# Masked attention, experts and feed-forward in one kernel: the first heads' loads in the order of their use, and the second head's bucket bits ahead of the others'

## The chip, the cores and the metric

The kernel runs on one core of one Trainium2 chip. The metric is the device time of one execution in microseconds (us): the median of three runs. The engines named here are PE (TensorE, matrix products), DVE (VectorE), ACT (ScalarE), POOL (GpSimd) and SP (SyncE, which issues most of the DMA transfers). Every engine works through a list of its own in a fixed order; an instruction that waits for a semaphore holds up all that stand behind it on its engine, and this holds for SP's list of DMA issues too.

## The reference

Three stages follow one another: attention with a mask from hashed buckets, a mixture of experts with one expert per token, and a dense feed-forward h·relu6(h+3)/6. Only the attention stage is touched by the change:

```python
# q, k, v: (2 batches, 8 heads, 768, 64); proj: (64, 6)
q_bits = (einsum('bhsd,dk->bhsk', q, proj) > 0)      # six bits a row
k_bits = (einsum('bhsd,dk->bhsk', k, proj) > 0)
mask   = q_bucket[:, :, :, None] == k_bucket[:, :, None, :]
scores = scale * q @ k.T
scores = where(mask, scores, -1e9)
scores = scores - max(scores, axis=-1)
attn   = exp(scores);  attn = attn / (sum(attn) + 1e-9)
return attn @ v
```

The 1536 rows of the result are the tokens; `x @ w_gate` picks one of 8 experts for each (512 to 1024 to 512, at most 384 tokens an expert), and the feed-forward (512 to 2048 to 512) comes last.

## The kernel before, in words

There are 16 heads (2 x 8), of 768 rows each. The attention stage has 96 steps, six of them for each head: step k handles one block of 128 keys against all 768 queries of its head. What a head needs stands in four tiles of a set (there are four sets, used in turn): X and Y on the side of the queries, K1 and K2 on that of the keys. The data are split in a high and a low half (`hi`, `lo`) for precision; rows 64 to 75 of X and K2 hold the bucket bits as +-numbers, so that a matching bucket adds a constant to the product, and row 76 holds the row's maximum against a row of -1.

Work of one head, in the order in which it is needed:

- `load_r(h)` (L308) loads q and k of a head, 393 kB. `prep(h)` makes `hi` on ACT (L319) and `lo` on DVE (L335), or for the heads in the table entry `ap` on ACT and POOL (L332, L333), and copies them by DMA from SBUF to SBUF into X and K2 (L321, L322) and K1 and Y (L325, L326, L336, L337).
- `bits(g)` handles the bits of four heads: dots with the projection into PSUM (`psb`, L358), signs on DVE into the tile `b` (L347). `put_bits(h)` copies them into X and K2 by two DMAs (L343, L344). Head 0 has its bits made apart at the start.
- `mx(n)` is one block of 128 rows for the row maxima: two matmuls (`psm`, L385) and two maxima on DVE (L388). After the sixth block of a head the six are reduced to `top` (L391), and a DMA sends it to X's row 76 (L392). A table (`ac`) says how many such blocks run ahead in the first steps.
- `scores(k)`: matmuls L402 and L403 into `pst`, exp on ACT (L404) to `pf`; then a high half on ACT (L412) and a low half on POOL (L418), and four steps later, for two steps together, `pv` (L430 to L432) into `psv`.
- For each group of four heads: `load_v(g)` (L510, 786 kB), the largest |v| on DVE (`vmax`, L514), and a power of two from it (`vscale`): the maxima `am` (L523, L525) are transposed on PE (`psn`, L531), reduced (L534) and laid on a diagonal (`dg`, L537), spread over the partitions by PE (`pso`, L540), and turned to scales on DVE (L544 to L559). The `sc` of it scales v (`vsplit`, L636 to L642), and the first call also scales the gate's weights `wg_sb` (L558).
- `load_vt(r)` (L480) loads v of two heads, transposed, into `vt`, of which there is one buffer; `vgate(r)` multiplies it with the scaled gate's weights on PE (`psg`, L491), read by DVE (L500, L501). The next `load_vt` waits for those matmuls.
- `heat` (L283) puts matmuls into the list that compute nothing that is used; the table entry `hn` says how many stand ahead of the steps and in each of the first eight.

The PSUM tiles of `psn`, `pso`, `psg` and later `psb` share one buffer; `psm` has three, `pst` two.

The order on every engine is that in which the program emits its instructions. The head of the stage is written out (its loads, head 0's bits and six blocks of maxima, the first `vscale`); for the 96 steps a table `Q` gives the step, in quarters, at which each part is due, and `spread(k, gen, d)` emits the parts of a generator from step k on, d steps apart. So the table and the written-out head set SP's list as well.

Of the kernel before, what the change touches and what calls it, by code (L numbers as in the profile page):

```python
# [9 lines left out]
F32 = mybir.dt.float32  # L10
F32R = mybir.dt.float32r
# [40 lines left out]
def moe_attention_kernel(ctx, tc, qk, v, vt, pj, wg, w1, w2, win, wout, out, cap):  # L52
    nc = tc.nc
    pe, act, dve, pool, sp = nc.tensor, nc.scalar, nc.vector, nc.gpsimd, nc.sync
# [3 lines left out]
    def opened(stack, name, bufs, side="left", **kw):  # L58
        return stack.enter_context(tc.tile_pool(name=name, bufs=bufs, side=side, reuse_waits="tile", **kw))

    def f32(t):
        return t.bitcast(F32)

    def run(gen):
        for _ in gen:
            pass
# [191 lines left out]
                )  # L258


    Q = {'v': (-3.25, -4.75, -1.75, -2.25), 'vg': (-4.5, -4.75), 'vgd': 1, 'pr': (-13.0, -12.75, -12.0, -12.5), 'prd': 0.6, 'b0': 7.75, 'b': 1.75, 'bd': 0.5, 'vm0': (8.0, 8.25, 10.75, 13.0), 'vm': (-0.5, 4.75, 7.0, 12.25), 'vs': 13.25, 'pa': 1.5, 'ev': 0.5, 'lvt': -5.0, 'v4': (2.0, 3.75, 4.0, 16.25), 'vg0': (1.85, -4.4, 7.75), 'p2': 3.5, 'lr': (0, 3, 1.5, 4.5), 'lv': 5.5, 'vsd': 0.75, 'ac': (0, 0, 2, 6, 7, 8, 9, 10), 'hd': (3, 5, 17), 'hn': (4, 4, 2, 2, 4, 3, 0, 0, 0), 'ap': (0,), 'h0': (7,), 'hl': (4,), 'l0': (), 'll': (1, 10), 'ht': (5, 9)}


    with ExitStack() as actx:
        pa = opened(actx, "pa", 1)
        pr = opened(actx, "pr", 6)
        ph = opened(actx, "ph", 1)
# [3 lines left out]
        ps_v = opened(actx, "ps_v", 2, space=PSUM)  # L271
# [31 lines left out]
        def misc(name):  # L303
            return ps_x.tile([P, 512], F32, tag="x", name=name)

        def load_r(h):
            rt[h] = pr.tile([P, S], F32, tag="r", name=f"r{h}")
            sp.dma_start(out=rt[h], in_=qk[h])  # L308

        def prep(h, first=False):  # L310
# [28 lines left out]
        def put_bits(h):  # L339
            st = sets[h % 4]  # L340
            b = b_t[h // 4]
            o = 32 * (h % 4)
            sp.dma_start(out=f32(st["X"])[D : D + 12], in_=f32(b)[o : o + 12])  # L343
            sp.dma_start(out=f32(st["K2"])[D : D + 12], in_=f32(b)[o + 12 : o + 24])  # L344

        def signs(out, ps, c):
            dve.tensor_scalar(out=out, in0=ps, scalar1=0.0, scalar2=c, op0=ALU.is_gt, op1=ALU.subtract)  # L347

        def bits(g, tiles=None):

            b_t[g] = ph.tile([P, S], F32R, tag="b", name=f"b{g}", bufs=2)
            ps = [None] * 2

            def dot(n, i):
                if i == 0:
                    ps[n] = tiles[n] if tiles else misc(f"psb{g}{n}")
                c = slice(n * HS, (n + 1) * HS)
                pe.matmul(  # L358
                    ps[n][32 * i : 32 * i + 32, :HS], pj_sb[:, 0:32], rt[4 * g + i][:, c], start=True, stop=True
                )  # L360

            def rows(n):
                signs(b_t[g][:, n * HS : (n + 1) * HS], ps[n][:, :HS], cst_sb[:, 0:1])

            if tiles:
                for i in range(4):
                    for n in range(2):
                        dot(n, i)
                    yield
            for n in range(2):  # L370
                if not tiles:
                    for i in range(4):
                        dot(n, i)
                    yield
                rows(n)
                if not tiles:
                    yield

        def mx(n):
            h, c = divmod(n, NC)  # L380
            st = sets[h % 4]
            mm = mxs[h % 2]
            for n in range(2):
                ps = ps_m.tile([P, 512], F32, tag="m", name=f"psm{h}{c}{n}")
                pe.matmul(  # L385
                    ps[:, :HS], st["X"][0:76, c::NC], st["K2"][0:76, n * HS : (n + 1) * HS], start=True, stop=True
                )
                dve.tensor_reduce(out=mm[:, c, n : n + 1], in_=ps[:, :HS], axis=AX.X, op=ALU.max)  # L388
            if c == NC - 1:

                dve.tensor_reduce(out=top[:, h], in_=mm, axis=AX.X, op=ALU.max)  # L391
                sp.dma_start(out=f32(st["X"])[76:77, :].rearrange("o (p c) -> o p c", c=NC), in_=f32(top)[:, h])  # L392

        def scores(k):
            h, j = divmod(k, NC)
# [82 lines left out]
        def load_vt(r):  # L478
            vt_t[r] = pt.tile([P, S], F32, tag="vt", name=f"vt{r}", bufs=1)
            sp.dma_start(out=vt_t[r], in_=vt[r])  # L480
# [169 lines left out]
        load_r(0)  # L650
        act.dma_start(out=pj_sb, in_=pj)
        dve.memset(wg_sb, 0.0)
        for h in range(1, 4):
            load_r(h)
        load_v(0)
        load_vt(0)
        for i in range(2):
            act.dma_start(out=wg_sb[i * D : (i + 1) * D, :, i], in_=wg[i * D : (i + 1) * D])
        st, r0 = sets[0], rt[0]
        dve.tensor_scalar(out=st["X"][0:D], in0=r0[0:D], scalar1=SC, scalar2=None, op0=ALU.mult)  # L660
        act.activation(st["K2"][0:D], r0[D:P], AF.Copy, scale=SC)
        pre = [prep(h, h == 0) for h in range(3)]
        for n in range(2):
            for i, t in enumerate(("X", "K2")):
                c = slice(n * HS, (n + 1) * HS)
                ps = (ps_m, ps_t)[i].tile([P, 512], F32, tag="mt"[i], name=f"psf{n}{i}")
# [4 lines left out]
                signs(st[t][D : D + 12, c], ps[D : D + 12, :HS], cst_sb[D : D + 12, i : i + 1])  # L671
        run(pre[0])
        next(pre[1])
        for i in range(4):
            pool.dma_start(out=f32(sets[i]["K2"])[76:77], in_=neg)
        consts()
        pool.dma_start(out=xd[0:1, :], in_=zrow[:, :DM])
        DOT = (5,)
        b0 = bits(0, [ps_v.tile([P, 512], F32, tag="v", name=f"psb0{n}") for n in range(2)])
        for n in range(NC):  # L680
            mx(n)
            if n in DOT:
                next(b0)
        heat(ps_t, "t", Q["hn"][0])
        for i in range(4):
            vmax(0, i)
        vs = vscale(0)
        next(vs)
        next(vs)
        run(b0)  # L690
        next(vs)
        put_bits(1)
        run(pre[1])
        next(pre[2])
        put_bits(2)

        heat_t.clear()
        STEPS = NC * NH
        AC = (0,) + Q["ac"]
        AHEAD = [range(NC + AC[i], NC + AC[i + 1]) for i in range(8)]  # L700
        END = 2 * NC

        def on_dve(k):
            if k < END:
                return k in Q["h0"]
            return k - STEPS + END in Q["hl"] if k >= STEPS - END else k % 24 in Q["hd"]
# [92 lines left out]
        h = NH - 1  # L799
# [229 lines left out]
    def heat(n):  # L1029
# [21 lines left out]
        out=gates, in0=ps2[:, :, NW:], scalar=1.0 / LS, in1=gates, op0=ALU.mult, op1=ALU.add  # L1051
# [288 lines left out]
```

## Time and profile before

| | us |
| --- | --- |
| median of the runs | 718.79 (717.63 to 719.08) |
| profiled execution, device time | 712.88 |
| its span in the profile | 711.1 |
| PE busy in that span | 682.9 (96%) |
| start of the first `scores` | 19.28 |
| start of the first `pv` | 40.36 |

The span is what the profile shows from the first instruction to the last, and all times of rows are counted from its start. The profiled execution lies 5.91 below the median of the timed runs. The mean granted TensorE clock is 0.983 of full speed. In the rows below a line like "14.10 1.92 DVE L514 ... x4" says that four instructions of line 514 began at 14.10 us and took 1.92 us together; the bracket at its end is the idle time of the engine before it, and who ended it. Rows with "SPq" are DMA issues: the time is that of the issue, not of the transfer.

### The profile page before, as it was taken

The numbers are of one execution on the slowest core, as the hardware profiler recorded it, in microseconds if no ns is written. First come the engines' busy times: TensorE is split into PE (matmuls) and PEld (weight loads), VectorE is DVE, ScalarE is ACT, GpSimd is POOL, SyncE is SP. The second block draws the span as 40 slices with busy tenths as digits, with TensorE's granted clock in tenths as the row PEclk, the third lists the DMA queues.
The fourth block names the chain that finished last, engine by engine and source line by source line (L and its number), as shares of the span: only waits on it lengthen the run. The fifth ranks groups of instructions, "written<-read, shape, count | busy, mean of one in ns | idle before, by whom it ended". The sixth has DMA issues, their size and how long they took to land. (4 is left out here: it accounts for less than half of the span.)

```text
span 711.1 us, 14232 instructions
## 1 busy us (share of the span) xinstructions
PE 682.9 (96%) x5528; PEld 598.2 (84%) x5528; DVE 503.5 (71%) x988; ACT 376.8 (53%) x713; POOL 260.6 (37%) x202
## 2 busy tenths in 40 slices
PE   7999999999998699999999998999999999999996
PEld 2689898898897489999999996788888888888885
DVE  6778889889999788778777785888888632222320
ACT  3468869778779366655666642333333442223420
POOL 4347877977982411110110001333333423311212
PEclk8789999999999999999999999999999999999999
DMA  7585855746480376666665543234333000000001
GB/s 224 120 227 130 239 141 156 226 127 167 98 230 25 115 238 223 218 208 209 209 213 189 193 150 123 89 128 137 121 119 118 1 17 29 30 16 1 0 30 59
DMA packets 37841, 94.14 MB, mean 132 GB/s; under 512 B 7576, under 2 KB 13720, under 8 KB 37760
## 3 DMA queue, kind: packets, MB, share of 16 engines
q1 hardware_dynamic: 34672, 85.71, 40.2%
q0 software_dynamic: 2400, 7.36, 3.1%
q8 instruction: 46, 0.75, 0.4%
q14 instruction: 35, 0.29, 0.1%
q10 hardware_dynamic: 688, 0.03, 0.1%
HBM read 67.14 MB, written 6.29 MB: 103 GB/s over the span
## 5 line engine op out<-in xcount | busy, mean ns | idle before, releaser
L418 POOL TENSOR_TENSOR plo<-pf,phi 128x768 f16<-128x768 f32 x86 | 146.7, 1728 | 60.6 <-ACT phi L412 25.9
L996 POOL TENSOR_TENSOR ib<-wi,ia 128x512 fp32r<-128x512 f32 x32 | 50.1, 1566 | 230.1 <-ACT ia L995 230.1
L388 DVE TENSOR_REDUCE mx<-psm 128x1 f32<-128x384 f32 x192 | 96.3, 548 | 20.1 <-PE psm L385 19.8
L404 ACT ACTIVATE pf<-pst 128x384 f32<-128x384 f32 x192 | 83.4, 486 | 48.9 <-PE pst L403 47.5
L135 DVE TENSOR_TENSOR wl<-raw,wh 128x512 fp32r<-128x512 f32 x128 | 86.7, 688 | 10.2 <-ACT wh L134 3.7
L1223 ACT ACTIVATE rl<-psg,b 128x512 f32<-128x512 f32 x64 | 37.3, 582 | 94.6 <-PE psg L1221 94.5
L1221 PE MATMUL psg<-yTh,ia 128*128 128x512 f32 (+1 forms) x256 | 86.4, 338 | 0.7 <-DVE rl L1224 0.2
L1224 DVE SCALAR_TENSOR_TENSOR rl<-rl,psg 128x512 f32<-128x512 f32 x64 | 35.1, 550 | 73.3 <-ACT rl L1223 73.3
L1221 PE MATMUL psg<-yTh,ib 128*128 128x512 f32 (+1 forms) x256 | 85.9, 335 | 0.0
L1221 PE MATMUL psg<-yTl,ia 128*128 128x512 f32 (+1 forms) x256 | 85.7, 335 | 0.0
L134 ACT ACTIVATE wh<-raw 128x512 fp32r<-128x512 f32 x128 | 77.3, 623 | 2.1 <-issue 1.5
L1243 PE MATMUL pso<-cl,gh 128*128 128x512 f32 x192 | 76.7, 399 | 0.5 <-POOL cl L996 0.5
L402 PE MATMUL pst<-Y,K 128*128 128x384 f32 x192 | 75.1, 391 | 2.0 <-ACT pf L404 2.0
L1243 PE MATMUL pso<-ch,gl 128*128 128x512 f32 x192 | 75.5, 393 | 0.0
L1243 PE MATMUL pso<-ch,gh 128*128 128x512 f32 x192 | 75.5, 393 | 0.0
L412 ACT ACTIVATE phi<-pf 128x768 f16<-128x768 f32 x85 | 71.7, 844 | 1.9
L978 PE MATMUL psy<-hh,wh 128*128 128x224 f32 x256 | 71.3, 279 | 0.0
L385 PE MATMUL psm<-K,X 76*128 76x384 f32 x192 | 66.8, 429 | 4.3 <-DVE mx L388 3.5
L978 PE MATMUL psy<-hl,wh 128*128 128x224 f32 x256 | 70.2, 274 | 0.0
L978 PE MATMUL psy<-hh,wl 128*128 128x224 f32 x256 | 70.1, 274 | 0.0
L403 PE MATMUL pst<-X,K 77*128 77x384 f32 x192 | 66.2, 345 | 0.0
L432 PE MATMUL psv<-vh,plo 128*128 128x73 f16 x576 | 63.6, 196 | 1.7 <-DVE plo L418 1.7
(204 smaller groups left out, 1642.6 us busy)
## 6 DMA issues: line engine op xcount, KB each, us to landing
raw<-in_w_dram SPq DMA_DIRECT2D x64, 512.0 KB
rc<-in_win_dram SPq DMA_DIRECT2D x16, 512.0 KB
rc<-in_wout_dram SPq DMA_DIRECT2D x16, 512.0 KB
r<-in_qk_dram SPq DMA_DIRECT2D x16, 384.0 KB
K<-hi SPq DMA_DIRECT2D x31, 192.0 KB
vr<-in_v_dram SPq DMA_DIRECT2D x4, 768.0 KB
vt<-in_vt_dram SPq DMA_DIRECT2D x8, 384.0 KB
Y<-hi SPq DMA_DIRECT2D x16, 192.0 KB
```

The lines of the kernel that those rows point to most:

```text
L134: act.activation(wh[e, i][:, c], r, AF.Copy)
L135: lo.tensor_tensor(out=wl[e, i][:, c], in0=r, in1=f32(wh[e, i])[:, c], op=ALU.subtract)
L385: pe.matmul(ps[:, :HS], st["X"][0:76, c::NC], st["K2"][0:76, n * HS : (n + 1) * HS], start=True, stop=True)
L388: dve.tensor_reduce(out=mm[:, c, n : n + 1], in_=ps[:, :HS], axis=AX.X, op=ALU.max)
L402: pe.matmul(ps[:, :HS], st["K1"][:, kc], st["Y"][:, qc], start=True, stop=False)
L403: pe.matmul(ps[:, :HS], st["K2"][0:77, kc], st["X"][0:77, qc], start=False, stop=True)
L404: act.activation(pf.rearrange("k (c n p) -> k c n p", c=NC, n=2)[:, :, n], ps[:, :HS].rearrange("k (p c) -> k c p", c=NC), AF.Exp, scale=0 ...
L412: act.activation(phi_t[k], pf_t[k], AF.Copy)
L418: eng.tensor_tensor(out=plo_t[k], in0=pf_t.pop(k), in1=phi_t[k], op=ALU.subtract)
L978: pe.matmul(ps, l, r, start=n == 0, stop=n == 3 * KF - 1)
L1221: pe.matmul(ps, l, x, start=n == 0, stop=n == 3 * KD - 1)
L1243: pe.matmul(po[blk][s], l, r, start=first and n == 0, stop=last and n == 2)
```

## The change

At the start only r of heads 0 and 1 is loaded; r of heads 2 and 3 and v of the first group are issued after head 0's K1 and Y and head 1's X and K2 copies, and the first transposed v after that of head 2's first part. At once after head 0's maxima the dots of head 1 alone are made and their bits sent; those of heads 2 and 3 are made from step 0.25 on (`bits` takes a range of heads), and head 2's are sent at step 2.5 (head 3's, as before, in its `prep`). `top` of head 0 is sent from ACT's queue. Head 1's `lo` moves from DVE to ACT and POOL. In the table, `vm0` (the maxima of v of the second group), `lr` (r of heads 4 to 7) and `lv` (v of the second group) become later, the parts of the first `vscale` stand half a step apart from step 0 on instead of being partly written out ahead, head 1's maxima begin a step earlier, and `hn` falls from 19 to 12 matmuls in all.

```diff
-Q: 'vm0': (8.0, 8.25, 10.75, 13.0), 'lr': (0, 3, 1.5, 4.5), 'lv': 5.5, 'vsd': 0.75, 'ac': (0, 0, 2, 6, 7, 8, 9, 10), 'hn': (4, 4, 2, 2, 4, 3, 0, 0, 0), 'ap': (0,)
+Q: 'vm0': (10.25, 11.0, 11.75, 13.0), 'lr': (2, 3.5, 4.5, 5.5), 'lv': 6.5, 'vsd': 0.5, 'ac': (0, 2, 4, 6, 7, 8, 9, 10), 'hn': (6, 2, 2, 1, 1, 0, 0, 0, 0), 'ap': (0, 1)
...
-        def bits(g, tiles=None):
+        def bits(g, heads=range(4), tiles=None):
...
+            p = slice(32 * heads[0], 32 * heads[-1] + 32)
...
             def rows(n):
-                signs(b_t[g][:, n * HS : (n + 1) * HS], ps[n][:, :HS], cst_sb[:, 0:1])
+                signs(b_t[g][p, n * HS : (n + 1) * HS], ps[n][p, :HS], cst_sb[p, 0:1])
...
-                sp.dma_start(out=f32(st["X"])[76:77, :].rearrange("o (p c) -> o p c", c=NC), in_=f32(top)[:, h])
+                (sp if h else act).dma_start(out=f32(st["X"])[76:77, :].rearrange("o (p c) -> o p c", c=NC), in_=f32(top)[:, h])
...
-        for h in range(1, 4):
-            load_r(h)
-        load_v(0)
-        load_vt(0)
+        load_r(1)
...
         next(pre[1])
+        load_r(2)
+        load_r(3)
+        load_v(0)
...
-        DOT = (5,)
-        b0 = bits(0, [ps_v.tile([P, 512], F32, tag="v", name=f"psb0{n}") for n in range(2)])
+        b0 = bits(0, [1], [ps_v.tile([P, 512], F32, tag="v", name=f"psb0{n}") for n in range(2)])
         for n in range(NC):
             mx(n)
-            if n in DOT:
-                next(b0)
+        run(b0)
+        put_bits(1)
+        run(pre[1])
         heat(ps_t, "t", Q["hn"][0])
         for i in range(4):
             vmax(0, i)
         vs = vscale(0)
         next(vs)
-        next(vs)
-        run(b0)
-        next(vs)
-        put_bits(1)
-        run(pre[1])
         next(pre[2])
-        put_bits(2)
+        load_vt(0)
...
         spread(0, vs, Q["vsd"])
+        spread(0.25, bits(0, [2, 3]), 0.5)
+        at(2.5, put_bits, 2)
```

Three places show how this moves instructions. SP's list at the start, before (r, vr, vt: loads of q and k, of v, of the transposed v; K, X, Y: the tiles of the sets; `b`: the bits):

```order
L308 DMA r_156<-in_qk_dram 128x768
L308 DMA r_160<-in_qk_dram 128x768
L308 DMA r_162<-in_qk_dram 128x768
L308 DMA r_164<-in_qk_dram 128x768
L510 DMA vr_166<-in_v_dram 128x1536
L480 DMA vt_169<-in_vt_dram 128x768
L325 DMA K_129<-hi_187 64x768
L326 DMA Y_128<-hi_187 64x768
```

and now:

```order
L325 DMA K_129<-hi_178 64x768
L326 DMA Y_128<-hi_178 64x768
L336 DMA K_129<-lo_179 64x768
L337 DMA Y_128<-lo_179 64x768
L321 DMA X_131<-hi_188 64x768
L322 DMA K_134<-hi_188 64x768
L308 DMA r_193<-in_qk_dram 128x768
L308 DMA r_195<-in_qk_dram 128x768
L510 DMA vr_197<-in_v_dram 128x1536
L343 DMA X_131<-b_262 12x768
```

The two loads of r and the load of v now stand behind six copies of 64x768 from SBUF to SBUF; ahead of these rows there are only r of heads 0 and 1. Further down SP's list, around the second load of the transposed v, before (X_135 and K_138 are head 2's X and K2):

```order
L326 DMA Y_136<-hi_300 64x768
L343 DMA X_135<-b_264 12x768
L344 DMA K_138<-b_264 12x768
L308 DMA r_325<-in_qk_dram 128x768
L480 DMA vt_354<-in_vt_dram 128x768
L308 DMA r_356<-in_qk_dram 128x768
L392 DMA X_131<-top 1x128x6
```

and now:

```order
L326 DMA Y_136<-hi_290 64x768
L480 DMA vt_297<-in_vt_dram 128x768
L480 DMA vt_346<-in_vt_dram 128x768
L308 DMA r_394<-in_qk_dram 128x768
L343 DMA X_135<-b_262 12x768
L344 DMA K_138<-b_262 12x768
L392 DMA X_131<-top 1x128x6
```

Head 2's bits stood ahead of the second load of `vt` and stand now behind it and behind one load of r. DVE's list in the first `vscale`, before:

```order
L534 TENSOR_REDUCE am_289<-psn_279 2x1
L537 TENSOR_TENSOR dg<-am_289,ident 2x2
L335 SCALAR_TENSOR_TENSOR lo_198<-r_160,hi_197 128x768
L544 COPY am_340<-pso_323 128x2
```

and now (`mx_148` are the maxima of head 1):

```order
L534 TENSOR_REDUCE am_316<-psn_311 2x1
L537 TENSOR_TENSOR dg<-am_316,ident 2x2
L388 TENSOR_REDUCE mx_148<-psm_333 128x1
L388 TENSOR_REDUCE mx_148<-psm_336 128x1
L388 TENSOR_REDUCE mx_148<-psm_339 128x1
L388 TENSOR_REDUCE mx_148<-psm_342 128x1
L347 TENSOR_SCALAR b_262<-psb_313,pj_sb 64x384
L544 COPY am_353<-pso_348 128x2
```

The second half of `vscale` (from L544 on) now stands behind four of head 1's twelve maxima and one half of the bits of heads 2 and 3; L335 of head 1 is gone.

## Rows read from the trace of the kernel before

**Rows 1.** The page: busy time of TensorE, share of the span, instructions.

```profile
PE 682.9 (96%) x5528; PEld 598.2 (84%) x5528; DVE 503.5 (71%) x988; ACT 376.8 (53%) x713; POOL 260.6 (37%) x202
```

**Rows 2.** Windows: length, busy time by engine, granted clock, DMA share, GB/s.

```profile
19.28:26.54 7.26, 5.60 (x29) 3.50 (x26) 6.76 (x17) 5.09 (x10) 3.43 (x2) 1.00 0.46 114
26.54:34.99 8.45, 8.44 (x29) 6.34 (x29) 5.87 (x14) 2.16 (x4) 3.29 (x2) 0.58 0.75 155
34.99:41.50 6.51, 6.51 (x36) 5.26 (x36) 4.10 (x10) 4.76 (x9) 1.65 (x1) 0.50 0.82 237
41.50:45.00 3.50, 3.50 (x44) 3.25 (x42) 2.55 (x7) 2.56 (x6) 2.14 (x2) 1.00 1.01 313
...
100.00:200.00 100.00, 98.17 (x1188) 89.23 (x1188) 88.42 (x203) 81.03 (x151) 81.96 (x55) 1.00 0.57 151
```

**Rows 3.** Windows of the first transfers: loads, then copies.

```profile
9.00:11.00 2.00, 2.00 (x5) 1.32 (x5) 2.00 (x5) 0.00 (x0) 1.93 (x5) 0.95 1.03 389
11.20:14.00 2.80, 2.80 (x7) 1.47 (x7) 2.77 (x6) 0.00 (x0) 2.05 (x12) 0.50 1.04 224
```

**Rows 4.** Timeline of SP: start, time of the issue, what is issued.

```profile
10.17 0.95 SPq L322 DMA_DIRECT2D K<-hi  x1
14.21 0.52 SPq L392 DMA_DIRECT2D X<-top  x1
...
21.57 0.74 SPq L344 DMA_DIRECT2D K<-b  x1
...
35.26 0.34 SPq L480 DMA_DIRECT2D vt<-in_vt_dram  x1
35.64 0.43 SPq L308 DMA_DIRECT2D r<-in_qk_dram  x1
```

**Rows 5.** Waits of SP from 13.9 to 45 us: total, times, longest.

```profile
SPq L480 <- PE psg L491: 5.4, 1, 5.4
```

**Rows 6.** Timeline of DVE.

```profile
14.10 1.92 DVE L514 TENSOR_REDUCE am<-vr 128x1 f32<-128x384 f32 x4
...
19.44 1.14 DVE L347 TENSOR_SCALAR b<-psb,pj_sb 128x384 fp32r<-128x384 f32 x2 [3.09 <-PE psb L358]
20.50 0.27 DVE L534 TENSOR_REDUCE am<-psn 2x1 f32<-2x128 f32 x1
...
21.08 0.96 DVE L335 SCALAR_TENSOR_TENSOR lo<-r,hi 128x768 fp32r<-128x768 f32 x1
21.96 0.15 DVE L544 COPY am<-pso 128x2 f32<-128x2 f32 x1
...
25.93 1.94 DVE L388 TENSOR_REDUCE mx<-psm 128x1 f32<-128x384 f32 x4
29.69 3.81 DVE L388 TENSOR_REDUCE mx<-psm 128x1 f32<-128x384 f32 x8 [1.81 <-PE psm L385]
33.53 0.17 DVE L391 TENSOR_REDUCE top<-mx 128x6 fp32r<-128x18 f32 x1
```

**Rows 7.** Timeline of PE.

```profile
13.27 2.77 PE L358 MATMUL psb<-r,pj_sb 128*32 128x384 f32 x4
...
17.85 1.50 PE L358 MATMUL psb<-r,pj_sb 128*32 128x384 f32 x12
...
23.93 0.98 PE L385 MATMUL psm<-K,X 76*128 76x384 f32 x3
26.54 0.56 PE L385 MATMUL psm<-K,X 76*128 76x384 f32 x1 [1.63 <-DVE mx L388]
...
35.06 0.67 PE L402 MATMUL pst<-Y,K 128*128 128x384 f32 x1
...
36.49 1.50 PE L283 MATMUL heatv<-idle_sb 128*128 128x512 f16 x3
37.44 1.20 PE L385 MATMUL psm<-K,X 76*128 76x384 f32 x2
...
40.36 0.28 PE L430 MATMUL psv<-vh,phi 128*128 128x73 f16 x1
```

More of the change, by code (lines that the diff above doesn't have):

```diff
@@ L258, in windows @@
                 )
-    Q = {'v': (-3.25, -4.75, -1.75, -2.25), 'vg': (-4.5, -4.75), 'vgd': 1, 'pr': (-13.0, -12.75, -12.0, -12.5), 'prd': 0.6, 'b0': 7.75, 'b': 1.75, 'bd': 0.5, 'vm0': (8.0, 8.25, 10.75, 13.0), 'vm': (-0.5, 4.75, 7.0, 12.25), 'vs': 13.25, 'pa': 1.5, 'ev': 0.5, 'lvt': -5.0, 'v4': (2.0, 3.75, 4.0, 16.25), 'vg0': (1.85, -4.4, 7.75), 'p2': 3.5, 'lr': (0, 3, 1.5, 4.5), 'lv': 5.5, 'vsd': 0.75, 'ac': (0, 0, 2, 6, 7, 8, 9, 10), 'hd': (3, 5, 17), 'hn': (4, 4, 2, 2, 4, 3, 0, 0, 0), 'ap': (0,), 'h0': (7,), 'hl': (4,), 'l0': (), 'll': (1, 10), 'ht': (5, 9)}
+    Q = {'v': (-3.25, -4.75, -1.75, -2.25), 'vg': (-4.5, -4.75), 'vgd': 1, 'pr': (-13.0, -12.75, -12.0, -12.5), 'prd': 0.6, 'b0': 7.75, 'b': 1.75, 'bd': 0.5, 'vm0': (10.25, 11.0, 11.75, 13.0), 'vm': (-0.5, 4.75, 7.0, 12.25), 'vs': 13.25, 'pa': 1.5, 'ev': 0.5, 'lvt': -5.0, 'v4': (2.0, 3.75, 4.0, 16.25), 'vg0': (1.85, -4.4, 7.75), 'p2': 3.5, 'lr': (2, 3.5, 4.5, 5.5), 'lv': 6.5, 'vsd': 0.5, 'ac': (0, 2, 4, 6, 7, 8, 9, 10), 'hd': (3, 5, 17), 'hn': (6, 2, 2, 1, 1, 0, 0, 0, 0), 'ap': (0, 1), 'h0': (7,), 'hl': (4,), 'l0': (), 'll': (1, 10), 'ht': (5, 9)}
     with ExitStack() as actx:
@@ L347, in signs @@
             dve.tensor_scalar(out=out, in0=ps, scalar1=0.0, scalar2=c, op0=ALU.is_gt, op1=ALU.subtract)
-        def bits(g, tiles=None):
-            b_t[g] = ph.tile([P, S], F32R, tag="b", name=f"b{g}", bufs=2)
+        def bits(g, heads=range(4), tiles=None):
+            if g not in b_t:
+                b_t[g] = ph.tile([P, S], F32R, tag="b", name=f"b{g}", bufs=2)
+            p = slice(32 * heads[0], 32 * heads[-1] + 32)
             ps = [None] * 2
             def dot(n, i):
-                if i == 0:
+                if i == heads[0]:
                     ps[n] = tiles[n] if tiles else misc(f"psb{g}{n}")
@@ L362, in rows @@
             def rows(n):
-                signs(b_t[g][:, n * HS : (n + 1) * HS], ps[n][:, :HS], cst_sb[:, 0:1])
[L365 to L369, printed above, removed]
-            for n in range(2):
[L371 to L375, printed above, removed]
+                signs(b_t[g][p, n * HS : (n + 1) * HS], ps[n][p, :HS], cst_sb[p, 0:1])
+            for n in range(2):
+                for i in heads:
+                    dot(n, i)
                 if not tiles:
                     yield
+                    rows(n)
+                    yield
+            if tiles:
+                yield
+                rows(0)
+                rows(1)
         def mx(n):
```

## The prediction

> **What bounds the kernel now.** I read the page first: PE is busy for 96% of the span [rows 1], so whatever moves the moment from which PE runs without waits moves the end. Then windows over the first 200 us, to see where that moment is. From 41.50 on PE is busy all the time at full clock, and still for 98.17 of 100 us between 100 and 200 us [rows 2]; before 41.50 it waits, or runs at the lower of its two levels (0.50 between 34.99 and 41.50). The change touches only this stretch. Behind it the lists of PE hold the same work in the same order, and its loads (r of heads 4 to 7, v of the second group) are used 20 and more steps after they are issued. So I ask by how much the first `pv` (40.36 [rows 7]) and what follows come later or sooner, and carry that to the end in full.
>
> Then the timelines of SP, DVE and PE side by side. The chain that leads to 40.36 goes through DVE: `vmax` of v at 14.10, bits at 19.44, `vscale`'s second half from 21.96 to 25.93, then the twelve maxima of head 1, up to its `top` at 33.53 [rows 6]. PE follows its last maxima with `vgate`, reaches step 4 at 35.06, and head 2's first maxima (`psm`) at 37.44 [rows 7]. SP, meanwhile, waited 5.4 us in the issue of the second `vt` for `vgate` [rows 5], until 35.26 [rows 4].
>
> **The change, part by part.**
>
> *v of the first group comes later.* Before, it stood fifth in SP's list, and `vmax` began at 14.10 without waiting. Now SP issues r2, r3 and v0 only after the copy of 10.17 (0.95 long [rows 4]), so from 11.12 on: 393 + 393 + 786 kB = 1.573 MB. At the 389 GB/s of the loads this is 4.0 us, at the 224 GB/s of the copies 7.0 [rows 3]. Earliest end: 11.12 + 4.0 = 15.1. Latest: 11.12 + 7.0 plus 1.6 for the start (below) = 19.7. I take the loads' rate, with 1.6 for the start and half a copy (197 kB at 224 GB/s is 0.9) in front: 17.2. DVE cannot begin before 16.7 anyway: the second dot of head 1 ends where the two dots of 13.27 do, at 16.04 [rows 7], and its eviction (0.57, half of the 1.14 for two [rows 6]; that one of 32 partitions takes as long is an estimate) ends near 16.7. So `vmax` begins at 17.2 (16.7 to 19.7) instead of 14.10.
>
> A rule speaks to this rate. The Trainium skill, "DMA: Bandwidth & Descriptors", section "Bandwidth", says that transfers between HBM and SBUF are bound by the HBM side and those inside SBUF by a faster fabric (some 435 GB/s). The trace has it the other way round: loads at 389, copies at 224 [rows 3]. By the page the copy in front would be gone 0.2 us sooner, and the sum below would be 0.2 less.
>
> *`vscale`, first half.* 17.2 + 1.92 [rows 6] + 0.4 for two small reductions (twice `top`'s 0.17) = 19.5. Transposing 0.3 (an estimate), then L534 and `dg` in 0.6 (20.50 to 21.08 [rows 6]): done at 20.4, which is 0.7 sooner than before, since the bits of heads 1 to 3 are no longer in front. The late v is paid out of a wait of 3.09 before the evictions [rows 6]. PE gets to the first scores at 16.04 + 6 heats of 0.32 (36.49 to 37.44, three [rows 7]) = 18.0, instead of 19.28, but that gains nothing, because PE then stands waiting for `am`.
>
> *`vscale`, second half.* This is the first loss. In DVE's list four maxima of head 1 and half of the bits now stand between `dg` and L544. In PE's list behind the transposition: two dots for heads 2 and 3 (the 1.50 for 12 records [rows 7] are two halves of three heads, so 0.75), step 1's scores 0.8 (step 4 at the low clock took 35.06 to 36.49, 1.43 [rows 7], about half at full), two heats 0.4, the first `psm` 0.4 (0.98 for three [rows 7]). So the first maximum at 19.5 + 0.3 + 2.35 = 22.2; four of them 1.94, half of the bits 0.57: 24.7. `pso` shares its PSUM buffer with `psb`, so it starts then; 0.6 for it and the way back: L544 at 25.3, not 21.96. From L544 to the end of the chain 3.97 (21.96 to 25.93 [rows 6]): 29.3. Eight maxima 3.81, the other half of the bits 0.57, and a gap for PE's scores of step 3: before it was 1.81 [rows 6], now the bits and one heat instead of four cover a part, I take 0.8 (0 to 1.8). With 0.1 for each of four hand-overs: `top` at 34.9 against 33.53, **+1.4**. L335 of head 1 (0.96 [rows 6]) is gone from DVE, but the two more evictions (1.14) have its place. On POOL, which did nothing there, `lo` is free; if POOL were late, K1's copies of head 1 still have until step 6. The ends: +0.1 (v0 in time, no gap) and +4.9 (v0 2.5 later, gap 1.8).
>
> *Head 2's bits.* This is the second loss, and a new wait. `vgate` follows head 1's last maxima as before, so step 4 begins 1.4 later too. Before, step 4 to head 2's first `psm` took 2.38, of which 0.95 were three heats (36.49 to 37.44 [rows 7]); those are now gone, but the copies of the bits, which had been issued long ahead, stand behind the second `vt`, and that waits for `vgate` [rows 5]. In the times of before: issue of `vt` at 35.26, r up to 36.07, then two bit copies of 0.74 each with 0.08 between [rows 4]: 37.7. The landing takes between nothing and 1.6: head 1's last copy ended its issue at 22.31 [rows 4], and its reader ran at 23.93 [rows 7]. In front of them lie 786 kB of `vt` and r, 2.0 us at 389 GB/s, 3.5 at 224 [rows 3]; begun 1.6 after 35.26 they are through at 38.9 or 40.4. So `psm` at 37.7 to 40.9; with the loads' rate and 0.3 for the bits' own 74 kB I take 39.2: **+1.8** (+0.3 to +3.5). Queued behind on SP: `top` of head 1 and `lo` of head 2, which are needed two steps later or more; on PE step 5 and the first `pv`.
>
> *The clock.* PE's clock was 1.00 from 19.28 to 26.54, 0.58 after it and 0.50 until 41.50, 1.1 us into `pv` [rows 2, 7]. With PE waiting near 39 the return may be later. If it comes as the first `pv` begins, 0.6 is gained; if all work up to 45 is done at half rate, 3.5 are lost [rows 2]. I take **+0.5**, near the end at which it comes as before.
>
> *Nothing else.* Sending `top` from ACT saves nothing: SP issued it at 14.21 [rows 4], at the end of the reduction, with nothing in front. The dropped heats stood in waits of PE, save the 0.95 counted. Later maxima for the second group and later r loads lie where DVE and DMA have room (DVE 88.42 of 100 [rows 2]).
>
> Sum: 1.4 + 1.8 + 0.5 = +3.7. On the profiled execution: 712.88 + 3.7 = 716.6; this lies 5.91 below the median of the runs, so the runs: 718.79 + 3.7 = 722.5.
>
> **The rivals.**
>
> *A larger loss, 725.5.* r2, r3 and v0 come at the copies' rate (+2.5), or the clock stays low past step 6 (+3). For it: both stretches of waiting are longer than before's, and the copies and loads are in the queues at the same time. Against it: at 9 to 11 us, in the same mix, 389 GB/s were moved [rows 3]. 3.7 + 3 = +6.7. The Trainium skill, same page, section "Rules for kernel authors", says to issue a DMA early and wait for it late; the change does the opposite for v0 and for head 2's bits, and 14.10, where `vmax` did not wait, agrees.
>
> *No change, 719.2.* v0 lands by 16.7, the bits as soon as issued, the clock as before: 0.1 + 0.3 + 0 = +0.4. Here belongs too that the change does less than it says, as with `top`'s queue. Against it: the issues alone take until 37.7.
>
> *Faster, 717.4.* The clock. The low stretch began after PE had waited 1.63 us for DVE ahead of 26.54 [rows 7]; if PE's new list, which starts scores 1.3 sooner and interleaves maxima with them, keeps 1.00 throughout, the 6.51 us of PE work from 34.99 to 41.50 [rows 2] shrink by 3.25, and `vgate` by some 1.3: 1.4 + 1.8 - 4.6 = -1.4. It decides at 27 to 35 us: the granted clock there must be 1.00. Against it: PE waits at 19, at 23 to 25 and before head 2's `psm`, with fewer heats in between.
>
> **How the numbers follow.** Forecast 0.56, with a range of its own of 720.7 to 724.5; larger loss 0.18; no change 0.14; faster 0.12. A difference of 0.2% (1.4 us) is about what a measurement of this kernel can tell from none. So slower 0.74, same 0.14, faster 0.12. The range for 8 in 10 reaches from 718.3, which leaves most of the faster case out, to 726.5, which leaves the tail of the larger loss out.
>
> **What would show it.** In the changed kernel's timelines: `vmax` starts at 16.7 to 18 behind a wait for the load of v; L544 at 25 to 26 with four maxima in front; SP issues the bits of head 2 after a `vt` that waited for `psg`, and PE stands for 2 us or more between step 4's scores and head 2's first `psm`; the first `pv` comes at 43 to 44.5, and from there PE is as busy as before. I am wrong if head 2's `psm` follows step 4 without a wait, if `vmax` starts before 16.7, or if the clock is 1.00 from 27 to 41 us.

## The result and the profile after

The changed kernel is slower: 726.25 us median beside 716.09 for the kernel before, in 20 runs of each; the ratio is 1.0134, with a 95% interval of 1.0116 to 1.0152. That is 9.6 us on 716.09 (8.3 to 10.9). The forecast was slower by 3.7, with 722.5 us, and a range of 718.3 to 726.5. Ratios go by the fast runs of each kernel, those within 1.5% of its fastest, and medians by all runs. So the direction held and the size did not: 3.7 of 9.6. That 726.25 still lies inside the stated range, by 0.25 us, is luck: the forecast was added to 718.79, and in these runs the kernel before came out 2.7 us lower. As a shift the range was -0.5 to +7.7, and the measured shift lies above it.

The profiled execution took 725.63 us (span 723.9, mean clock 0.976). On its page PE is busy for 686.6 us, 3.7 more than before [rows 1], at 95% of a longer span. Windows show where PE loses time and at which clock it works (length; PE, PEld, DVE, ACT, POOL busy; clock; DMA share; GB/s):

```profile
19.28:26.54 7.26, 4.59 (x15) 2.17 (x16) 3.68 (x8) 2.21 (x5) 1.64 (x1) 0.78 0.90 214
26.54:34.99 8.45, 6.43 (x20) 3.82 (x18) 4.18 (x16) 2.89 (x6) 1.64 (x1) 0.70 0.19 55
34.99:41.50 6.51, 6.49 (x23) 5.29 (x22) 5.00 (x12) 2.48 (x4) 3.28 (x2) 0.50 0.00 0
...
45.00:50.00 5.00, 3.15 (x15) 2.88 (x16) 2.00 (x6) 1.84 (x4) 1.64 (x1) 0.50 0.84 258
50.00:55.00 5.00, 5.00 (x80) 4.74 (x78) 4.09 (x11) 3.58 (x7) 2.98 (x2) 0.93 0.92 255
```

From 19.28 to 26.54 PE works 4.59 us, at 0.78, where before it had 5.60 at 1.00 [rows 2]; the low clock lasts until 50, not until 41.50. From 50 us on PE is as busy as before.

SP's timeline has the late loads, and the second new wait (start, time of the issue):

```profile
10.90 1.78 SPq L308 DMA_DIRECT2D r<-in_qk_dram  x2
12.73 0.43 SPq L510 DMA_DIRECT2D vr<-in_v_dram  x1
...
24.45 17.68 SPq L480 DMA_DIRECT2D vt<-in_vt_dram  x2
...
43.56 0.76 SPq L344 DMA_DIRECT2D K<-b  x1
```

SP's waits have the reason for the second (total, times, longest):

```profile
SPq L480 <- PE psg L491: 13.0, 1, 13.0
```

and before, the same copy of head 2's bits was issued without such a wait:

```profile
28.43 0.77 SPq L344 DMA_DIRECT2D K<-b  x1
```

The two loads of r take from 10.90 to 12.68 to issue, v follows at 12.73. The pair of `vt` issues stands from 24.45 to 42.13: the second waits 13.0 us for `vgate`, and head 2's bits come behind it, with K's copy at 43.56 instead of 28.43. Between 11 and 17 us the transfers run at 226 to 351 GB/s, not at the 389 of 9 to 11 us before [rows 3]:

```profile
11.00:13.00 2.00, 2.00 (x6) 1.34 (x5) 2.00 (x5) 0.00 (x0) 1.87 (x13) 1.00 0.88 226
13.00:15.00 2.00, 2.00 (x5) 0.65 (x5) 1.36 (x5) 0.01 (x1) 0.43 (x1) 1.00 0.87 238
15.00:17.00 2.00, 2.00 (x6) 0.35 (x5) 1.19 (x2) 1.15 (x2) 1.08 (x1) 1.00 0.95 351
```

DVE's timeline answers to [rows 6]:

```profile
20.37 1.93 DVE L514 TENSOR_REDUCE am<-vr 128x1 f32<-128x384 f32 x4 [3.51 <-DMA vr<-in_v_dram]
...
23.47 1.18 DVE L537 TENSOR_TENSOR dg<-am,ident 2x2 f32<-2x2 f32 x1
27.35 1.95 DVE L388 TENSOR_REDUCE mx<-psm 128x1 f32<-128x384 f32 x4 [2.71 <-PE psm L385]
...
30.60 0.16 DVE L544 COPY am<-pso 128x2 f32<-128x2 f32 x1 [0.66 <-PE pso L540]
30.79 0.17 DVE L548 TENSOR_SCALAR am<-am 128x2 int32<-128x2 int32 x1
...
34.70 1.95 DVE L388 TENSOR_REDUCE mx<-psm 128x1 f32<-128x384 f32 x4 [2.61 <-PE psm L385]
...
40.08 0.17 DVE L391 TENSOR_REDUCE top<-mx 128x6 fp32r<-128x18 f32 x1
```

`vmax` waited 3.51 us for v and began at 20.37 instead of 14.10. `dg` stood 1.18 us; L544 comes at 30.60 instead of 21.96; L548 took 0.17 (1.44 before); `top` of head 1 comes at 40.08 instead of 33.53. PE's timeline answers to [rows 7]:

```profile
20.67 0.41 PE L403 MATMUL pst<-X,K 77*128 77x384 f32 x1 [2.71 <-DMA X<-top]
...
22.78 0.27 PE L531 MATMUL psn<-ident,am 128*2 128x128 f32 x1 [0.91 <-DVE am L525]
23.42 1.50 PE L360 MATMUL psb<-r,pj_sb 128*32 128x384 f32 x4 [0.37 <-DVE am L534]
...
30.81 1.49 PE L360 MATMUL psb<-r,pj_sb 128*32 128x384 f32 x4 [0.25 <-DVE am L544]
...
41.61 0.67 PE L402 MATMUL pst<-Y,K 128*128 128x384 f32 x1
...
46.85 0.99 PE L385 MATMUL psm<-K,X 76*128 76x384 f32 x2 [3.61 <-DMA X<-top]
```

L403 of the first scores stood 2.71 us for the copy of `top`, which ACT had issued at 14.39. This was hidden: PE then had to wait for `am` until 22.78 all the same. Each half of the bits of heads 2 and 3 took 1.5 us. Step 4 began at 41.61 (35.06 before), and head 2's first `psm`, after 3.61 us of waiting for copies, at 46.85 (37.44 before). The label names a copy of `top` into an X tile; this `psm` reads head 2's X and K2, whose last copies are the bits, issued just before that `top`, and a_vt1 below shows that it stood for them. Then the shift stays:

```profile
49.56 0.28 PE L430 MATMUL psv<-vh,phi 128*128 128x73 f16 x1
...
61.83 1.41 PE L491 MATMUL psg<-wg_sb,vt 128*128 128x16 f32 x12
```

and before:

```profile
52.68 1.41 PE L491 MATMUL psg<-wg_sb,vt 128*128 128x16 f32 x12
```

The first `pv` is 9.2 us later (49.56 and 40.36 [rows 7]), and the second `vgate` (step 10) is 9.15 us later. That agrees with the 9.6 of the timed runs. The two spans differ by more (12.8): what comes after the second `vgate` is 662.1 us in this execution and 658.4 in that of before, and between 658 and 667 in the profiles of the kernels below, though what stands in PE's lists there is nearly the same. So for the experiments the timed ratio and the second `vgate` are read, not the span.

### The profile page after: what moved, and what is told of

Its sections match the earlier page's. It is cut to its first block, busy times and chain, and to the rows that moved or that the text cites. A ratio compares the mean times of both kernels' runs of the same rounds, so it can differ in the third digit from the quotient of the medians.

```text
span 723.9 us, 14213 instructions
## 1 busy us (share of the span) xinstructions
PE 686.6 (95%) x5517; PEld 599.5 (83%) x5517; DVE 502.7 (69%) x989; ACT 378.0 (52%) x714; POOL 262.0 (36%) x203
## 5 line engine op out<-in xcount | busy, mean ns | idle before, releaser
L403 PE MATMUL pst<-X,K 77*128 77x384 f32 x192 | 67.5, 351 | 2.7 <-DMA X<-top 2.7
```

The costliest lines, as they stand in the source:

```text
L403: pe.matmul(ps[:, :HS], st["K2"][0:77, kc], st["X"][0:77, qc], start=False, stop=True)
```

## The experiments

The kernels below were timed in five rounds against the kernel before, with 12 runs each (b_loads 6) beside 23 to 35 of before. The times in the table are starts in each profile. For the kernels slower than before the second `vgate` and the timed ratio agree within 1.5 us; for those that are as fast or faster they differ by up to 3.7 us (a_best: 0.26 us sooner in the profile, 4.0 in the timed runs), so there the profile does not show where the gain lies.

| kernel | ratio to before (95%) | `vmax` | L544 | `top` of head 1 | first `pv` | second `vgate` |
| --- | --- | --- | --- | --- | --- | --- |
| before | 1 | 14.10 | 21.96 | 33.53 | 40.36 | 52.68 |
| changed | 1.0134 (1.0116 to 1.0152) | 20.37 | 30.60 | 40.08 | 49.56 | 61.83 |
| a_vt1 | 1.0052 (1.0022 to 1.0082) | 19.22 | 29.46 | 38.94 | 44.47 | 57.01 |
| a_loads | 1.0058 (1.0034 to 1.0083) | 17.34 | 25.91 | 34.74 | 44.44 | 57.55 |
| a_v0 | 1.0078 (1.0047 to 1.0109) | 17.15 | 26.21 | 35.70 | 45.27 | 58.65 |
| a_both | 1.0001 (0.9975 to 1.0028) | 17.02 | 25.59 | 34.50 | 40.02 | 53.30 |
| b_loads | 1.0099 (1.0068 to 1.0131) | 20.53 | 28.89 | 40.97 | 48.27 | 61.14 |
| b_acttop | 0.9983 (0.9956 to 1.0010) | 14.29 | 22.52 | 33.61 | 39.97 | 53.29 |
| b_vsfirst | 0.9953 (0.9919 to 0.9987) | 14.40 | 18.35 | 31.69 | 38.12 | 52.27 |
| b_best | 0.9974 (0.9947 to 1.0002) | 14.70 | 19.05 | 32.85 | 36.12 | 52.33 |
| a_best | 0.9944 (0.9915 to 0.9974) | 14.57 | 20.87 | 34.26 | 37.84 | 52.42 |
| a_best2 | 1.0018 (0.9980 to 1.0056) | 14.31 | 19.78 | 31.20 | 37.25 | 50.48 |

**a_vt1: head 2's bits ahead of the second `vt`.**

```diff
-                at(NC * h + Q["lvt"], load_vt, h // 2 + 1)
+                at(2.75 if h == 1 else NC * h + Q["lvt"], load_vt, h // 2 + 1)
```

> The changed kernel with the second load of vt issued behind head 2's bits and head 1's top (step 2.75 instead of 1). If head 2's bits are held up by that load's wait for vgate, as the trace of the changed kernel suggests, head 2's first psm follows step 4's scores at about 43 us instead of 46.85, and the time falls by 3.5 to 5 us from 726.25 (5 to 6.5 us above before). The rival: the wait only moves, to the landing of the copies or to the lo of head 2; then less than 1 us is gained.

Measured: 719.89 us, 1.0052. Of the 1.34% above before 0.82% are gone, 5.9 us, somewhat more than the 3.5 to 5 expected. SP issues the second `vt` last, and PE goes from step 4 to head 2's `psm` without a wait:

```profile
40.67 0.33 SPq L480 DMA_DIRECT2D vt<-in_vt_dram  x1
```

```profile
40.48 0.67 PE L402 MATMUL pst<-Y,K 128*128 128x384 f32 x1
...
41.91 0.84 PE L385 MATMUL psm<-K,X 76*128 76x384 f32 x2
```

Step 4 to `psm` takes 1.43 us, where the changed kernel takes 5.24 and before 2.38. The wait did not move elsewhere, so the rival falls. In this one execution v came 1.1 us sooner too, so of the 4.8 us by which the second `vgate` is earlier (61.83 to 57.01) 3.8 are the wait's.

**a_loads: the old loads at the start.**

```diff
-        load_r(1)
+        for h in range(1, 4):
+            load_r(h)
+        load_v(0)
+        load_vt(0)
...
-        load_r(2)
-        load_r(3)
-        load_v(0)
...
-        load_vt(0)
```

> The changed kernel with all first loads at the start again, in the order of before (r1, r2, r3, v0, vt0); the rest as changed. Theory: the late v of the first group is the largest single loss; vmax begins near 16.9 us instead of 20.37, the wait of the first scores for X<-top (2.71) is gone, and the time falls by 3.5 to 5 us. Rival: the place of vscale's second half behind the maxima is the largest loss and swallows the earlier v; L544 moves by less than 1.5 us from 30.60 and the time by 0 to 1.5 us.

Measured: 721.24 us, 1.0058, so 5.4 us less than the changed kernel: a little more than the theory's upper end, and far from the rival's. On DVE, and then on PE:

```profile
17.34 1.93 DVE L514 TENSOR_REDUCE am<-vr 128x1 f32<-128x384 f32 x4
```

```profile
20.39 0.84 PE L360 MATMUL psb<-r,pj_sb 128*32 128x384 f32 x4 [0.37 <-DVE am L534]
...
41.73 0.99 PE L385 MATMUL psm<-K,X 76*128 76x384 f32 x2 [3.83 <-DMA X<-b]
```

`vmax` no longer waits (the 17.34 is DVE's own, behind the bits of head 1), L544 moved by 4.7 us, and a half of the bits takes 0.84 at full clock. The wait for head 2's bits is there as before (3.83).

**a_v0: of the late loads only v early.**

```diff
         load_r(1)
+        load_v(0)
...
         load_r(3)
-        load_v(0)
```

> The changed kernel with v of the first group alone loaded at the start, behind r of heads 0 and 1; r2, r3 and vt0 stay late, head 2's bits stay behind the second vt. Theory: of the late loads it is v that costs, and the first scores' wait for X<-top (2.71 us) is its companion, since that small copy lies in the same transfer engines as 1.57 MB of loads: vmax near 17, the wait for X<-top under 0.5, time as with all old loads (4 to 5 us above before). Rival: r2 and r3 cost as much, through the dots of heads 2 and 3 or the queue in front of X<-top; then 6 to 8 us above before.

Measured: 721.80 us, 1.0078. That is 5.6 us above before (3.4 to 7.8), between the 4 to 5 of the theory and the 6 to 8 of the rival. `vmax` and `top` stand within 1 us of a_loads, and no wait for X<-top is left:

```profile
18.86 0.34 PE L403 MATMUL pst<-X,K 77*128 77x384 f32 x1
```

By the ratios v alone gives back 4.0 of the 5.4 us. Whether late r2 and r3 add the 1.4 us between the two kernels cannot be told, since the intervals overlap.

**b_loads: the kernel before with the late loads alone.**

```diff
-        for h in range(1, 4):
-            load_r(h)
-        load_v(0)
-        load_vt(0)
+        load_r(1)
...
         next(pre[1])
+        load_r(2)
+        load_r(3)
+        load_v(0)
...
         put_bits(2)
+        load_vt(0)
```

> The kernel before with the later loads alone (r2, r3, v0 behind the six copies, vt0 behind head 2's first part). If the late loads cost by themselves: vmax near 20.4 us, dots of heads 2 and 3 wait for r3, L544 at 25 to 27 instead of 21.96, time 4 to 7 us above before. If the wait of 3.09 us on DVE ahead of the bits hides most of it: L544 below 24 and the time 0 to 2 us above before.

Measured: 724.10 us, 1.0099, so 7.1 us (4.9 to 9.4): the late loads cost by themselves. That is a little more than the 5.4 of the changed kernel, though the intervals overlap; in the profile the difference is that all twelve dots of heads 1 to 3 stand behind `psn` here:

```profile
20.53 1.93 DVE L514 TENSOR_REDUCE am<-vr 128x1 f32<-128x384 f32 x4 [6.17 <-DMA vr<-in_v_dram]
...
27.18 0.27 DVE L534 TENSOR_REDUCE am<-psn 2x1 f32<-2x128 f32 x1
```

```profile
22.94 0.37 PE L531 MATMUL psn<-ident,am 128*2 128x128 f32 x1 [5.17 <-DVE am L525]
```

DVE waited 6.17 us for v and PE 5.17 for `am`; then the dots and the bits came, and L534 ran at 27.18, not 20.50 [rows 6]. L544 came at 28.89, later than the 25 to 27 expected, though the dots did not wait for r3. This trace also shows how v arrives, since SP issues nothing between the small copy of `top` at 14.39 and 27.30 (windows as above):

```profile
17.50:18.00 0.50, 0.27 (x2) 0.00 (x0) 0.00 (x0) 0.00 (x0) 0.00 (x0) 1.00 0.70 250
...
19.50:20.00 0.50, 0.00 (x0) 0.00 (x0) 0.00 (x0) 0.00 (x0) 0.00 (x0) 1.00 0.06 25
```

The transfers are nearly through at 18.0; from there they use 0.14 of their time, then 0.06, and `vmax` begins only at 20.53. So 2.5 us pass between the end of the bulk and the reader's start.

**a_both: both edits.** The diffs of a_vt1 and a_loads together.

> The changed kernel with both edits, old loads at the start and the second vt behind head 2's bits. If the two losses are all there is beside the clock, they add: 0 to 2 us above before. If the order of vscale, bits and maxima costs by itself, 4 us or more above before remain, and in the trace L544 still stands at 26 us or later.

Measured: 716.90 us, 1.0001 (0.9975 to 1.0028), level with before. The two edits take 5.9 and 5.4 us by themselves and 9.5 together. That they share some 2 us is no more than the noise: by the intervals each of these differences is uncertain by some 2.5 us. So beside the two losses nothing is left that these runs can tell from none. Its L544 still stands at 25.59, near the 26 of the second theory, and yet no loss remains:

```profile
20.12 1.55 DVE L537 TENSOR_TENSOR dg<-am,ident 2x2 f32<-2x2 f32 x1
...
25.59 0.16 DVE L544 COPY am<-pso 128x2 f32<-128x2 f32 x1 [0.53 <-PE pso L540]
```

From L544 to `top` it took 8.91 us, where before took 11.57. The small instructions from L544 to L559 take 1.49 instead of 3.97, since L548 and L554 are short here (below), and four of head 1's maxima (1.95) stand ahead of L544; longer gaps and half of the bits take some 1.8 of this back. So `top` and step 4 (36.03) come only 1.0 later than before, and the three heats (0.95) that stood ahead of head 2's `psm` before and are gone here pay for that.

The same lists of PE and DVE run in this kernel and in the changed one from `dg` to L544. It took 3.92 us here (21.67 to 25.59) and 5.95 in the changed kernel (24.65 to 30.60), with the dots of a half of the bits at 0.84 (20.07) and 1.50, and with granted clocks of 1.00 and 0.79 in these stretches, here and in the changed kernel:

```profile
21.67:25.59 3.92, 2.12 (x9) 1.43 (x8) 2.58 (x5) 1.60 (x3) 1.64 (x1) 1.00 1.01 223
```

```profile
24.65:30.60 5.95, 4.14 (x14) 2.79 (x12) 2.58 (x6) 1.83 (x3) 1.64 (x1) 0.79 0.60 147
```

That is 2.0 us; counted from L531 ahead of it (19.43 and 22.78) it is 1.7, since `dg` itself stood 0.37 longer here.

**b_acttop: `top` of head 0 from ACT.**

```diff
-                sp.dma_start(out=f32(st["X"])[76:77, :].rearrange("o (p c) -> o p c", c=NC), in_=f32(top)[:, h])
+                (sp if h else act).dma_start(out=f32(st["X"])[76:77, :].rearrange("o (p c) -> o p c", c=NC), in_=f32(top)[:, h])
```

> The kernel before with one edit: top of head 0 is sent from ACT's queue. Theory: it costs and saves nothing, since SP issued it at 14.21 with nothing in front; the issue stands at 14.2 to 14.4 on ACT, the first scores at 19.3, and the time within 1 us of before. Rival: ACT's queue lands it sooner or later than SP's, or ACT's hi of head 2 behind it matters; then the first scores or pf move by 0.5 us or more and the time by more than 1 us.

Measured: 716.15 us, 0.9983 (0.9956 to 1.0010): no difference that can be told. The first scores came at 19.83 in this execution, 0.55 later than before, which is the rival's 0.5, but neither `top` of head 1 (33.61) nor the time followed.

**b_vsfirst: `vscale` ahead of the bits of heads 1 to 3, in the kernel before.**

```diff
-        heat(ps_t, "t", Q["hn"][0])
         for i in range(4):
             vmax(0, i)
         vs = vscale(0)
         next(vs)
+        heat(ps_t, "t", 2)
+        next(vs)
+        heat(ps_t, "t", 2)
         next(vs)
-        run(b0)
         next(vs)
+        next(vs, None)
+        run(b0)
```

> The kernel before with vscale as a whole ahead of the dots and bits of heads 1 to 3 (two heats, psn, two heats, pso, then the dots). Theory: L548 and L554 took 1.44 and 1.48 us in before because they stood until POOL's two plo ended (23.59 beside 23.56, 25.61 beside 25.58); with no such work on POOL they take 0.17 each, as in the changed kernel, dg stands near 17.4, L544 near 18.2, the first maximum of head 1 near 24 instead of 25.93, and the time is 1.5 to 3 us below before. Rival: the maxima of head 1 wait for PE and the bits' copies instead, and the time stays within 1 us.

Measured: 714.96 us, 0.9953 (0.9919 to 0.9987), faster by 3.4 us (0.9 to 5.8). In before, DVE's L548 and L554:

```profile
22.15 1.44 DVE L548 TENSOR_SCALAR am<-am 128x2 int32<-128x2 int32 x1
...
24.13 1.48 DVE L554 TENSOR_SCALAR sc<-ex 128x3 int32<-128x3 int32 x1
```

and POOL beside them:

```profile
21.78 1.78 POOL L418 TENSOR_TENSOR plo<-pf,phi 128x768 f16<-128x768 f32 x1 [8.40 <-ACT phi L412]
23.93 1.65 POOL L418 TENSOR_TENSOR plo<-pf,phi 128x768 f16<-128x768 f32 x1 [0.38 <-ACT phi L412]
```

L548 ends at 23.59 and `plo` at 23.56, L554 at 25.61 and `plo` at 25.58. With `vscale` where POOL has no such work, both take 0.17, and the chain from L544 to the first maximum is no longer what head 1 waits for:

```profile
18.55 0.17 DVE L548 TENSOR_SCALAR am<-am 128x2 int32<-128x2 int32 x1
...
19.26 0.17 DVE L554 TENSOR_SCALAR sc<-ex 128x3 int32<-128x3 int32 x1
...
24.87 1.95 DVE L388 TENSOR_REDUCE mx<-psm 128x1 f32<-128x384 f32 x4 [3.02 <-PE psm L385]
```

PE sets the first maximum now (24.87), and `top` comes 1.84 us sooner. The theory held for L548, L554 and the chain, and a part of the rival's wait is there too. In this profile the gain is down to 0.41 us at the second `vgate` (52.27), so where the 3.4 us of the timed runs lie is not shown.

**a_best and a_best2: the changed kernel with both edits, and `vscale` ahead of the first scores.** To a_both it adds:

```diff
-'vsd': 0.5
+'vsd': 0.25
...
-                rows(0)
+                rows(0); yield
...
-        run(b0)
+        next(b0)
+        vmax(0, 0)
+        next(b0)
+        vmax(0, 1)
+        run(b0)
...
-        heat(ps_t, "t", Q["hn"][0])
-        for i in range(4):
-            vmax(0, i)
+        vmax(0, 2)
+        vmax(0, 3)
         vs = vscale(0)
         next(vs)
+        heat(ps_t, "t", 3)
+        next(vs)
+        heat(ps_t, "t", 3)
+        next(vs)
+        next(vs)
...
-        spread(0.25, bits(0, [2, 3]), 0.5)
+        spread(0.75, bits(0, [2, 3]), 0.5)
```

> The changed kernel with both edits (old loads, second vt behind head 2's bits), the maxima of v between the two evictions of head 1's bits, and psn, dg and pso ahead of the first scores. If the changed order of bits is good in itself once v is early: dg near 18.7, L544 near 20, step 4 near 33 to 34 instead of 35.06, 2 to 4 us below before. If splitting the bits gains nothing: within 1 us of before.

Measured: 712.85 us, 0.9944 (0.9915 to 0.9974): faster than both kernels, by 4.0 us than before (1.9 to 6.1). Step 4 began at 34.54, between the 35.06 of before and the 33 to 34 expected. PE's clock is 1.00 from 14 to 34.99, where before had 0.58 in the last 8.45 us of it [rows 2]:

```profile
26.54:34.99 8.45, 8.06 (x42) 5.61 (x43) 6.98 (x15) 3.82 (x7) 4.40 (x3) 1.00 0.25 64
```

But the first `pv` is only 2.5 us sooner, and PE then waits for an r:

```profile
47.00 0.83 PE L360 MATMUL psb<-r,pj_sb 128*32 128x384 f32 x2 [1.42 <-DMA r<-in_qk_dram]
```

so that the second `vgate` stands 0.26 us before that of before. The rest of the 4.0 isn't to be seen in this one execution, and is left open. In a_best2 the loads of heads 4 to 7 came earlier:

```diff
-'lr': (2, 3.5, 4.5, 5.5), 'lv': 6.5
+'lr': (0, 0.5, 1, 1.5), 'lv': 3.5
```

> The kernel of a_best with r of heads 4 to 7 at steps 0, 0.5, 1 and 1.5 and v of the second group at 3.5. In a_best the transfers are nearly idle from 26.5 to 35 us (share 0.25) and PE waits 1.42 us for an r at 47. Theory: loads moved into that gap take this wait away, and the second vgate comes 1 to 2 us sooner than 52.4; 4 to 6 us below before. Rival: they get in front of head 2's bits and hold its first psm; then as fast as before or slower.

Measured: 719.37 us, 1.0018 (0.9980 to 1.0056): as before. The expected gain is there in the profile's execution (second `vgate` at 50.48), and so is its rival, head 2's `psm` waiting 2.11 us for its bits behind the loads:

```profile
34.54 0.99 PE L385 MATMUL psm<-K,X 76*128 76x384 f32 x2 [2.11 <-DMA K<-b]
```

The runs, from 712.19 to 726.62, lie further apart than those of a_best (711.4 to 717.76), and the profiled execution was the fastest of them, so this profile doesn't explain the median. Why they are apart stays open.

**b_best: before, with `vscale` ahead, head 1's `lo` on ACT and POOL, and head 1's maxima a step earlier.** To b_vsfirst it adds the entries

```diff
-'ac': (0, 0, 2, 6, 7, 8, 9, 10), 'hn': (4, 4, 2, 2, 4, 3, 0, 0, 0), 'ap': (0,)
+'ac': (0, 2, 4, 6, 7, 8, 9, 10), 'hn': (4, 4, 3, 3, 2, 2, 0, 0, 0), 'ap': (0, 1)
```

> The same with head 1's lo on ACT and POOL, head 1's maxima a step earlier (ac of the changed kernel) and heats 4, 4, 3, 3, 2, 2. Theory: three parts of the change that cost nothing are kept, and PE has fewer waits between 19 and 40 us; first pv near 36 to 38 instead of 40.36, 3 to 5 us below before. Rival: it is the waits for head 2's bits or the low clock that set 40.36; then no more than 1 us below before.

Measured: 715.54 us, 0.9974 (0.9947 to 1.0002): 1.9 us below before, not clear of noise and short of the forecast. The first `pv` did come at 36.12, 4.2 us sooner, at full clock (1.00 from 26.54 to 41.50); but nearly all of it was given back before step 10 (second `vgate` 52.33):

```profile
41.50:50.00 8.50, 6.07 (x89) 4.77 (x85) 4.21 (x8) 3.81 (x7) 1.40 (x1) 1.00 0.98 232
```

```profile
48.61 1.01 DVE L514 TENSOR_REDUCE am<-vr 128x1 f32<-128x384 f32 x2 [2.61 <-DMA vr<-in_v_dram]
```

From 41.5 to 50 us the transfers are at 0.98 of their time, PE works 6.07 of 8.50 us, and DVE waits 2.61 us for v of the second group. In this execution, behind an earlier start, the loads are the next bound.

## Why the prediction was right in its direction and short in its size

- *PE sets the end, and a shift of the first `pv` lasts.* Right: 9.2 us at the first `pv`, 9.15 at the second `vgate`, 9.6 in the timed runs. A reason given beside it was wrong: that the loads of heads 4 to 7 and of the second v are used 20 and more steps after their issue. The table has the first dots on heads 4 to 7 at step 7.75 and the maxima of the second v from step 8 (10.25 in the changed kernel) on. In the changed kernel no engine's wait came of it, but where the start is earlier PE and DVE stand for these loads (1.42 us in a_best, 2.61 in b_best).
- *v of the first group lands at 17.2 (16.7 to 19.7).* This step failed most. It landed at 20.37, past the range's end. I took the loads' 389 GB/s [rows 3] for r2, r3 and v; between copies, beside which they now ran, the rate was 226 to 238 for the first four microseconds, and 226 is near the copies' rate that I kept for the end of the range. The second part is the landing, for which I had 1.6. In b_loads, where SP issues nothing of size behind these loads, the bulk is through at 18.0 instead of 15.6, 2.4 us late, and `vmax` follows after 2.5 us, 0.9 more than I had. By the rule of the Trainium skill that was weighed there ("DMA: Bandwidth & Descriptors", section "Bandwidth") the copy in front would have been shorter by an estimated 0.2 us; the trace does not agree with it, with 226 to 238 here as with the 224 of [rows 3].
- *`dg` is 0.7 sooner than before all the same.* It was done at 24.65, 3.6 later than before and 4.25 later than forecast (20.4): 3.2 from v, and 1.0 because `dg` stood for POOL's `plo`, 23.00 to 24.64:

```profile
23.00 1.64 POOL L418 TENSOR_TENSOR plo<-pf,phi 128x768 f16<-128x768 f32 x1 [5.27 <-ACT phi L412]
```

- *L544 at 25.3.* It came at 30.60. From `dg` 5.95 us instead of 4.9, since PE ran the part ahead of the maxima at the lower clock (0.79 granted on average).
- *L544 to the chain's end 3.97.* This cost was too large: 1.5, since POOL was idle there. I had read the 1.44 and 1.48 of before as the instructions' own time.
- *A gap of 0.8 before the second four maxima, `top` +1.4.* The gap was 2.61: between the two groups PE also has the second half of the bits (1.49), which I counted on DVE and forgot on PE, and another 0.79 stood before the last four. From L544 to `top` it took 9.48 us, and I had 9.6: this sum came out by luck, because the chain's 2.5 too many make up for the gaps' 2.6 too few. `top` came 6.55 later. a_loads, with the loads early and the rest unchanged, has it 1.2 later (34.74): the +1.4 was nearly right for a v at 17.2, and the miss is the arrival of v (3.2) with `dg` (1.0) and the low clock behind it (1.05 beyond the 4.9).
- *Head 2's bits, +1.8.* Right mechanism, shown by a_vt1, and the size too small, though inside its own range (+0.3 to +3.5): step 4 to `psm` took 5.24 instead of 2.38, +2.9. The issues came as forecast; the reader ran 2.5 us after the last of them had ended (44.32 to 46.85), and I had 1.5 for that (37.7 to 39.2).
- *The clock, +0.5 after step 4.* From head 2's `psm` to the first `pv` took 2.71, beside 2.92 before: nothing was lost there. What the clock took lay ahead of it, 1.7 to 2.0 us up to L544 (a_both).
- *`top` from ACT: nothing.* Right (b_acttop). That the small copy would then wait behind the loads (2.71 us on PE) I had not seen; it cost nothing, as PE waited longer for `am`.
- *The rivals.* "A larger loss" named late data (+2.5) and was the nearest, +6.7 beside 9.6; that its 725.5 is so near 726.25 owes 2.7 us to the lower median of before. "Faster" needed a clock of 1.00 from 27 to 35, where 0.70 was granted.
- *The signs.* PE's wait ahead of head 2's `psm` (3.61) and the late issue of its bits came as named; `vmax` (20.37), L544 (30.60) and the first `pv` (49.56) all came later than the stretches that were named for them.

## What to carry to other kernels

A load that is put behind other transfers should be priced at the rate of that mixture, with the measured time from the end of the bulk to the reader (2.5 us here) on top, and its reader's arrival carried through every list behind it; here 3.2 us too little in one arrival, with what followed from it, were most of the miss. Look for each issue that stands behind one that waits: two small copies behind a load that waited for PE cost about as much (5.9 us) as 1.6 MB of loads that came late (5.4). And before a slow small instruction is taken at its traced duration, compare its end with that of what ran on the neighbour engine.

## What the runs showed of the hardware

Three small DVE instructions whose operands lie in SBUF stood until a GpSimd tensor operation was over: L548 1.44 us and L554 1.48 (before), and `dg` 1.18 (changed), each ending within 0.03 us of `plo`; they took 0.15 to 0.17 us without it (b_vsfirst, a_best). The Trainium skill, "SBUF — State Buffer", section "SBUF: two separate sides", says that GpSimd shares one pair of ports with certain DVE instructions, those with two SBUF inputs among them (as `dg`), and that whichever starts first holds the pair for its whole instruction; these rows agree.

A copy of 3 KB from ACT's queue, issued at 14.39 behind 1.6 MB of loads that SP had issued, let its reader (L403) run at 20.67; with the loads early the same reader ran at 18.08 (a_loads), and with only v early at 18.86 (a_v0), without that wait.
